# The second product of a fused attention and MoE kernel: from chunks of 512 tokens in one pass to chunks of 1024 tokens in two passes

## The chip, the cores and the metric

The kernel runs on one core of one Trainium2 chip. The metric is the time of one execution on the device in microseconds (us); the median of three runs before the change is 1302.53 us (1302.04 to 1304.47). Five engines work beside each other, each in its own program order: PE multiplies matrices into PSUM (eight banks of 128 x 512 fp32), VectorE (DVE), ScalarE (ACT) and GpSimd (POOL) work element by element, and SP issues the transfers between the chip's memory and SBUF.

## The reference

```python
def _moe_ref(x, w_in, w_out):                   # x: 4608 tokens x 512, from attention
    h = x @ w_in                                # 4608 x 2048
    sp = np.where(h > 20.0, h, np.log1p(np.exp(np.minimum(h, 20.0))))
    g = h * np.tanh(sp)                         # Mish
    return (g @ w_out).astype(np.float32)       # 4608 x 512
```

Ahead of it stands an attention over 8 batches, 8 heads and 576 positions that keeps only scores within tau of each row's maximum. All is fp32 at the door. The change touches only the last line, `g @ w_out`, and the preparation of `w_out`.

## The kernel before

**Three stages.** Attention and the first product (`x @ w_in`) run interleaved until 881 us or so; the last batch of the first product follows, beside the preparation of `w_out`; from 932 us on PE does the second product alone. The change concerns this last stage, and the preparation ahead of it.

**Number format.** An fp32 factor is held as two fp32r tiles, an upper part (a CAST on ACT) and the rest (a subtraction on DVE). A product is three matmuls: upper by upper, upper by rest, rest by upper. So `gh` and `gl` are the two parts of g, `w2h` and `w2l` of w_out, `sh` and `sl` of sums of w_out's blocks.

**The second product** (lines 966 to 1015) is a loop of `NG` = 72 steps n = (chunk c, j). Step j takes two blocks of 128 hidden features, j and j + 8. The output is made transposed: 512 output features by tokens. Chunk 0 (n < 8) is a plain product of 512 tokens: 24 matmuls of 512 moving columns a step, four banks. Each of the chunks 1 to 8 also has 512 tokens, as two halves of 256; with two halves of the features and two of the output this is a 2 x 2 by 2 x 2 block product, done in Winograd's way with seven products (`PRODUCTS`) in place of eight. Each product is 256 output features by 256 tokens: two groups of 128, three matmuls of 256 moving columns each, into one bank. So a step is 42 matmuls, and seven of the eight banks are in use. `leave` (line 935) takes each product out of its bank at j = 7, when its sum is complete, with running sums in SBUF tiles `c`, and writes four quarters of the output.

**What a step prepares for later steps**, ahead of its own matmuls in each engine's program order (lines 968 to 976):

- `combine(n + 3)`: ACT applies Mish to the loaded h in `z`; DVE makes two differences of 128 x 256 in one instruction, POOL two more of 128 x 256 after it.
- `split_z(n + 2)`: ACT casts seven blocks (128 x 1792) to `gh`, DVE subtracts to `gl`. Three pairs of tiles are used in turn, so this waits until PE has ended step n - 1.
- `load_z(n + 6)`: SP loads z, 2 transfers of 256 KB, into one of five buffers.

**The preparation of w_out**, for j = 0 to 7: `load_w` (two transfers), `convert`, `compose` (DVE and POOL join the two words of the 64 bit numbers), `upper_w` (one ACT cast of 128 x 1024), `lower_w` (one DVE subtraction of 128 x 1024), `sums_w` and `split_w`.

Instructions on PE, DVE, ACT and POOL stand in the order in which the code makes them (class `InOrder`); SP's order is set by the scheduler. Nearly all of them are recorded at line 77, so the profile's rows are told apart by tile names.

Of the kernel before, what the change touches and what calls it, by code (L numbers as in the profile page):

```python
# [62 lines left out]
def fv(ap):  # L63
    return ap.bitcast(F32)
# [78 lines left out]
def attention_moe(tc, q, k, v, tau, w_in, w_out, out):  # L143
# [3 lines left out]
    with ExitStack() as outer:  # L147
# [22 lines left out]
        def scratch(i, name):  # L170

            if i < 3:
                return homes["zp"].tile([P, 2048], F32, name=name, tag=f"b{(i + 1) % 3}")
            return homes["er"].tile([P, 2048], F32, name=name, tag=f"b{i}")

        def load_w(j):
            y = scratch(j % 3, "w").bitcast(U32)
            words[j] = y.rearrange("p (n t) -> p n t", t=2)
            for e in range(2):
                f = j + e * NJ  # L180
                nc.sync.dma_start(
                    words[j][:, e * DM:(e + 1) * DM],
                    w_out[f * P:(f + 1) * P].bitcast(U32).rearrange("p (n t) -> p n t", t=2),
                )

        def convert(j):
# [3 lines left out]

        def compose(j):
            top, low = words[j][:, :, 1], words.pop(j)[:, :, 0]
            wa[j] = [homes["wr"].tile([P, 4 * QT], F32R, name=f"w2h{j}")]
            a, b = (homes["wr"].tile([P, 4 * QT], U32, name=n, tag=f"{n}l{j}") for n in "as")
            whole[j] = fv(b)
            nc.vector.tensor_scalar(fv(b), fv(top), TOP_MAX, -TOP_MAX, ALU.min, ALU.max)
            nc.vector.tensor_scalar(a, b, 3, 0x7FFFFFF8, ALU.logical_shift_left, ALU.bitwise_and)
            nc.vector.scalar_tensor_tensor(b, b, 0x80000000, a, ALU.bitwise_and, ALU.bitwise_or)
            nc.gpsimd.tensor_tensor(b, b, low, ALU.add)

        def upper_w(j):
            nc.scalar.copy(wa[j][0], whole[j])

        def lower_w(j):
            wa[j].append(homes["wr"].tile([P, 4 * QT], F32R, name=f"w2l{j}", tag=f"al{j}"))
            nc.vector.tensor_tensor(wa[j][1], whole[j], fv(wa[j][0]), ALU.subtract)

        def sums_w(j):
            y = z[j]
            a11, a21, a12, a22 = (whole[j][:, i * QT:(i + 1) * QT] for i in range(4))  # L210
            nc.vector.tensor_tensor(y[:, 4], a21, a22, ALU.add)
            nc.vector.tensor_tensor(y[:, 6], a21, a11, ALU.subtract)
            nc.vector.tensor_tensor(y[:, 5], y[:, 4], a11, ALU.subtract)
            nc.vector.tensor_tensor(y[:, 7], a12, y[:, 5], ALU.subtract)

        def split_w(j):
# [5 lines left out]
            nc.scalar.copy(ws[j][0], y)  # L222
            nc.vector.tensor_tensor(ws[j][1], y, fv(ws[j][0]), ALU.subtract)

        def load_z(n):
            if n < NG:
                c, j = divmod(n, NJ)
                z[n] = scratch(CYCLE[n % 5], "z").rearrange("p (n t) -> p n t", t=QT)
                if c == 0:
                    for i in range(2):  # L230
                        nc.sync.dma_start(z[n][:, i:4:2], hd[i][:, j])
                else:
                    for at, i in ((0, 2 * c + 1), (2, 2 * c)):
                        nc.sync.dma_start(z[n][:, at:at + 2], hd[i][:, j])

        def combine(n):
            if n < NG:
                y = z[n]
                nc.scalar.activation(y[:, :4], y[:, :4], AF.Mish)
                if n >= NJ:  # L240
                    nc.vector.tensor_tensor(
                        y[:, 4:6], y[:, :1].to_broadcast([P, 2, QT]), y[:, 1:3], ALU.subtract
                    )
                    nc.gpsimd.tensor_tensor(y[:, 6], y[:, 1], y[:, 5], ALU.subtract)
                    nc.gpsimd.tensor_tensor(y[:, 7], y[:, 6], y[:, 3], ALU.subtract)

        def split_z(n):
            if n < NG:
                home = homes[("er", "wl", "wl")[n % 3]]
                gs[n] = [home.tile([P, 7, QT], F32R, name=f"g{m}", tag=f"g{m}{n % 3}") for m in "hl"]  # L250
                y = z[n][:, :4] if n < NJ else z.pop(n)[:, 1:]
                to = [x[:, :4] if n < NJ else x for x in gs[n]]
                nc.scalar.copy(to[0], y)
                nc.vector.tensor_tensor(to[1], y, fv(to[0]), ALU.subtract)

        nc = Engines(tc)
        with ExitStack() as first:
# [671 lines left out]
        def held():  # L929
            pair = hp.tile([P, 2, 2, QT], F32, name="c", tag="hst")  # L930
            return pair[:, 0], pair[:, 1]

        sums = {}

        def leave(k, c, o):

            def put(value, n, half):
                at = (2 * c + half) * QT
                nc.sync.dma_start(places[:, 2 * n:2 * n + 2, at:at + QT], value)

            def add(to, a, b, op=ALU.add):
                nc.vector.tensor_tensor(to, a, b, op)

            if k == 0:
                sums["c"], sums["u"] = held()
                nc.scalar.copy(sums["c"], o)
            elif k == 1:
                add(sums["u"], o, sums["c"])
            elif k == 2:
                sums["v"], sums["value"] = held()  # L950
                add(sums["v"], o, sums["u"])
            elif k == 3:
                add(sums["value"], o, sums["v"])
                put(sums["value"], 1, 1)
                add(sums["u"], o, sums["u"])
            elif k == 4:
                add(sums["u"], o, sums["u"])
                put(sums["u"], 0, 1)
            elif k == 5:
                add(sums["v"], sums["v"], o, ALU.subtract)  # L960
                put(sums["v"], 1, 0)
            else:
                add(sums["c"], o, sums["c"])
                put(sums["c"], 0, 0)

        for n in range(NG):
            c, j = divmod(n, NJ)
            combine(n + 3)
            for i in range(n + 1 + (n > 0), n + 3):
                split_z(i)  # L970
# [3 lines left out]
                split_w(i)  # L974
            for i in range(n + 5 + (n > 0), n + 7):
                load_z(i)
            if j == 0:
                banks = [bank("o") for _ in range(4 if c == 0 else len(PRODUCTS))]
            if c == 0:
                gh, gl = (x.rearrange("p n t -> p (n t)") for x in gs.pop(n))  # L980
                wh, wlo = wa[j]
                order = [(e, d) for e in range(2) for d in range(ND)]
                if j == NJ - 1:
                    order.sort(key=lambda at: at[1])
                for e, d in order:
                    cols = slice(2 * e * QT + d * P, 2 * e * QT + (d + 1) * P)
                    toks = slice(2 * e * QT, 2 * (e + 1) * QT)
                    for i, (x, y) in enumerate(((wh, gh), (wh, gl), (wlo, gh))):
                        nc.tensor.matmul(
                            banks[d], x[:, cols], y[:, toks],  # L990
                            start=j == e == i == 0, stop=j == NJ - 1 and e == 1 and i == 2,
                        )
                    if j == NJ - 1 and e == 1:
                        if d % 2 == 0:
                            pair = [x.rearrange("p n t -> p (n t)") for x in held()]
                        value = pair[d % 2]
                        if d % 2:
                            nc.vector.tensor_copy(value, banks[d])
                        else:
                            nc.scalar.copy(value, banks[d])  # L1000
                        nc.sync.dma_start(out[d * P:(d + 1) * P, :2 * QT], value)
                continue
            for k, (wi, gi) in enumerate(PRODUCTS):
                o = banks[k].rearrange("p (n t) -> p n t", t=QT)
                w, at = (wa[j], (0, 2, 3)[wi]) if wi < 3 else (ws[j], wi - 3)
                for b in range(2):
                    cols = slice(at * QT + b * P, at * QT + (b + 1) * P)
# [54 lines left out]
```

## Time and profile before

| what | value |
|---|---|
| the profiled execution, time | 1302.35 us |
| its span | 1300.6 us |
| granted TensorE clock | 1.00 |
| second product, first to last matmul | 931.97 to 1295.29 us |
| chunks 1 to 8 of it | from 978.27 us |
| DMA traffic over the span | 163 GB/s |

Of the 1.75 us between span and time the profile shows nothing. A row of the timeline gives start, duration, engine, line, operation, output <- inputs and form; idle time ahead of it and what ended that stand in brackets. A matmul's duration is the way of one through the array; they overlap, so that the distance of starts is the rate. A row of the windows gives for each engine the busy time and the number of instructions.

### The profile page before, as it was taken

How to read it: one execution, taken by the hardware profiler on the slowest of the kernel's cores; microseconds unless marked ns; L12 is line 12 of the kernel's file. 1: busy time of each engine (PE TensorE's matmuls, PEld its weight loads, DVE VectorE, ACT ScalarE, POOL GpSimd, SP SyncE). 2: the span in 40 equal slices, each digit the busy share in tenths (PEclk: the TensorE clock that was granted, in tenths of full speed). 3: DMA queues.
4: the chain of work that ended last, by engine and by line, in shares of the span. 5: the costliest groups of instructions: out<-in, count | busy, mean ns of one | idle time of the engine just before them, and what ended most of it. 6: DMA issues, size and time to landing. Idle time of an engine off the chain costs nothing.

```text
span 1300.6 us, 28613 instructions
## 1 busy us (share of the span) xinstructions
PE 1269.9 (98%) x9761; PEld 1137.0 (87%) x9761; DVE 991.5 (76%) x2590; ACT 842.4 (65%) x1620; POOL 776.2 (60%) x1071
## 2 busy tenths in 40 slices
PE   8789999999999999999999999999999999999998
PEld 6446998898888889889888888989889999999998
DVE  5888867777787888888888788859976676666664
ACT  5887877777866666676676666645755555655552
POOL 3778897787776786686677678624313433344331
PEclk9999999999999999999999999999999999999999
DMA  6444564777556566566655656547644444344440
GB/s 182 124 145 124 153 188 132 209 212 230 153 172 204 175 177 197 162 181 202 181 185 177 208 164 188 158 139 245 208 140 136 143 134 136 116 138 142 135 131 33
DMA packets 168802, 213.26 MB, mean 164 GB/s; under 512 B 27088, under 2 KB 140496, under 8 KB 163536
## 3 DMA queue, kind: packets, MB, share of 16 engines
q1 hardware_dynamic: 168656, 211.44, 53.4%
q8 instruction: 77, 1.26, 0.4%
q14 instruction: 69, 0.57, 0.1%
HBM read 151.62 MB, written 59.77 MB: 163 GB/s over the span
## 4 chain that ended last, share of the span: by engine, by line
PE 80%; DVE 8%; ACT 5%; issue 3%; POOL 2%; DMA 1%; DVEq 0%; POOLq 0%; ACTq 0%; SPq 0%
PE o L77 27%; PE h L77 22%; PE y L77 11%; PE s L77 10%; PE tp L77 8%; DVE st L77 3%; ACT e L77 2%; DVE p L77 1%; PE t L77 1%; DVE w2l L77 1%; DVE hst L77 1%; DVE s L77 1%; ACT dec L77 1%; ACT xh L77 0%; DVE a L77 0%
## 5 line engine op out<-in xcount | busy, mean ns | idle before, releaser
L77 DVE SCALAR_TENSOR_TENSOR p<-s,st,e 128x576 f32<-128x576 f32 x288 | 234.6, 815 | 103.5 <-ACT e L77 101.6
L77 POOL TENSOR_SCALAR p<-p,st 128x576 f32<-128x576 f32 x288 | 244.6, 849 | 98.0 <-DVE st L77 73.4
L77 POOL TENSOR_TENSOR z<-z 128x256 f32<-128x256 f32 x128 | 124.4, 976 | 223.0 <-DVE z L77 214.2
L77 ACT ACTIVATE e<-s,st 128x576 f32<-128x576 f32 x288 | 215.7, 749 | 55.4 <-DVE st L77 52.4
L77 PE MATMUL s<-k,q 128*128 128x288 f32 (+1 forms) x1280 | 228.7, 326 | 13.9 <-DVE p L77 13.6
L77 DVE TENSOR_REDUCE st<-s 128x1 f32<-128x576 f32 x288 | 217.1, 754 | 26.4 <-PE s L77 25.8
L77 DVE TENSOR_TENSOR gl<-z,gh 128x1792 fp32r<-128x1792 f32 (+1 forms) x72 | 141.6, 1968 | 108.2 <-ACT gh L77 108.2
L77 ACT CAST gh<-z 128x1792 fp32r<-128x1792 f32 (+1 forms) x72 | 116.5, 1620 | 149.9 <-issue 81.1
L77 PEld LDWEIGHTS s<-k,q 128*128 128x128 f32 (+1 forms) x1280 | 169.7, 188 | 45.4 <-DVE p L77 33.4
L77 PE MATMUL h<-xh,w1h 128*128 128x288 f32 x624 | 188.8, 302 | 0.0
L77 PE MATMUL h<-xl,w1h 128*128 128x288 f32 x624 | 184.2, 295 | 0.0
L77 PE MATMUL h<-xh,w1l 128*128 128x288 f32 x624 | 183.8, 295 | 0.0
L77 PE MATMUL tp<-ident,p 128*128 128x128 f32 x1152 | 175.2, 275 | 5.1 <-POOL p L77 3.6
L77 PE MATMUL h<-xh,wt 128*128 128x288 f32 x640 | 156.5, 305 | 3.4 <-ACT hst L77 3.4
L77 PEld LDWEIGHTS tp<-ident,p 128*128 128x128 f32 x1152 | 137.1, 140 | 24.5 <-issue 7.8
L77 PE MATMUL o<-gh,sl 128*128 128x256 f32 x512 | 144.5, 282 | 0.0
L77 PE MATMUL o<-gl,sh 128*128 128x256 f32 x512 | 143.8, 281 | 0.0
L77 PE MATMUL o<-gh,sh 128*128 128x256 f32 x512 | 143.5, 280 | 0.0
L77 PE MATMUL y<-hi,vf 128*64 128x320 f32 (+1 forms) x512 | 139.6, 413 | 0.0
L77 PE MATMUL y<-lo,vf 128*64 128x320 f32 (+1 forms) x512 | 139.6, 413 | 0.0
L77 ACT COPY hi<-tp 128x512 f32<-128x512 f32 (+1 forms) x160 | 87.2, 545 | 78.0 <-PE tp L77 76.3
L77 PE MATMUL o<-gl,w2h 128*128 128x256 f32 (+1 forms) x448 | 133.3, 298 | 1.3 <-DVE gl L77 1.3
(79 smaller groups left out, 3215.8 us busy)
## 6 DMA issues: line engine op xcount, KB each, us to landing
wt<-sw SPq DMA_DIRECT2D x40, 1024.0 KB, 5.9
z<-hd SPq DMA_DIRECT2D x144, 256.0 KB, 3.1
r<-q SPq DMA_DIRECT2D x108, 160.0 KB, 2.3
r<-k SPq DMA_DIRECT2D x108, 160.0 KB, 2.7
hd<-hst SPq DMA_DIRECT2D x60, 256.0 KB, 6.0
vf<-v SPq DMA_DIRECT2D x64, 160.0 KB, 3.5
out_t<-c SPq DMA_DIRECT2D x36, 256.0 KB, 2.4
dec<-w_in SPq DMA_DIRECT2D x16, 512.0 KB, 3.9
```

Source lines behind the costliest of these rows:

```text
L77: made = method(*args, **kwargs)
```

## The change

Chunks 1 to 4 of 1024 tokens take the place of chunks 1 to 8 of 512. Each token half now has 512 tokens, so a product is 256 output features by 512 tokens and needs two banks: 14 banks in all, of eight. The seven products are therefore done in two passes over the eight j, first four (`PASSES[0]`, the early pass), then three (`PASSES[1]`, the late pass). Products 5 and 6 of the late pass are added in PSUM onto what products 3 and 0 of the early pass left in theirs, so these four banks are kept; the other four are emptied between the passes. The number of steps stays 72: an early step has 24 matmuls of 512 columns, a late one 18.

An early step needs three of the four blocks of z (768 KB in four transfers) and four operands, a late one four blocks (1024 KB in four transfers) and three operands; Mish and the combination run for both passes. In an early combine DVE makes one difference of 128 x 512 and POOL two after it; in a late one POOL makes two and DVE a sum after them. The fourth operand's rest in an early step has a tile of its own, `ge`, and a DVE instruction of its own. `leave` now works on halves of a bank, 128 x 256, in SBUF tiles that held the upper parts of one quarter of w_out (`w2q`), which is not needed after step 7; product 6 is copied out by ACT into three `value` tiles. w_out is loaded in four transfers for each j, its upper part made by two ACT casts, its rest by DVE (768 columns) and POOL (256).

```diff
-PRODUCTS = ((0, 1), (4, 5), (5, 3), (3, 4), (6, 0), (2, 6), (1, 2))
+PASSES = (((0, 0, 2), (1, 4, 1), (2, 5, 0), (3, 3, 3)), ((4, 6, 0), (5, 2, 1), (6, 1, 2)))
...
         def upper_w(j):
-            nc.scalar.copy(wa[j][0], whole[j])
+            nc.scalar.copy(wa[j][0], whole[j][:, QT:])
+            nc.scalar.copy(wa[j][1], whole[j][:, :QT])
...
-            nc.vector.tensor_tensor(wa[j][1], whole[j], fv(wa[j][0]), ALU.subtract)
+            nc.vector.tensor_tensor(low[:, QT:], whole[j][:, QT:], fv(hi), ALU.subtract)
+            nc.gpsimd.tensor_tensor(low[:, :QT], whole[j][:, :QT], fv(quarter), ALU.subtract)
...
+        def place(n):
+            c, r = divmod(n - NJ, 2 * NJ)
+            return (c, *divmod(r, NJ))
...
+        def combine(n):
+            if NJ <= n < NG:
+                y = z[n]
+                if place(n)[1]:
+                    nc.scalar.activation(y, y, AF.Mish)
+                    nc.gpsimd.tensor_tensor(y[:, 0], y[:, 1], y[:, 0], ALU.subtract)
+                    nc.gpsimd.tensor_tensor(y[:, 2], y[:, 2], y[:, 3], ALU.subtract)
+                    nc.vector.tensor_tensor(y[:, 2], y[:, 2], y[:, 0], ALU.add)
                 else:
+                    nc.scalar.activation(y[:, :3], y[:, :3], AF.Mish)
+                    nc.vector.tensor_tensor(y[:, 3], y[:, 0], y[:, 2], ALU.subtract)
+                    nc.gpsimd.tensor_tensor(y[:, 0], y[:, 0], y[:, 1], ALU.subtract)
+                    nc.gpsimd.tensor_tensor(y[:, 1], y[:, 1], y[:, 3], ALU.subtract)
...
+            if place(n)[1]:
+                gs[n] = [[x[:, i] for i in range(3)] for x in (gh, gl)]
+                nc.scalar.copy(gh[:, :3], y[:, 1:])
+                nc.vector.tensor_tensor(gl, y[:, 1:], fv(gh[:, :3]), ALU.subtract)
+                return
...
+            nc.scalar.copy(gh, y)
+            nc.vector.tensor_tensor(gl, y[:, :3], fv(gh[:, :3]), ALU.subtract)
+            nc.vector.tensor_tensor(extra[n % 3], y[:, 3], fv(gh[:, 3]), ALU.subtract)
...
+        def leave(k, b, c, o):
+            for h in range(2):
+                x = o[:, h * QT:(h + 1) * QT]
+                us, vs = ("u", b, h), ("v", b, h)
...
+                if k == 0:
+                    kept[us] = spare(2 * b + h)
+                    nc.scalar.copy(kept[us], x)
+                elif k == 1:
+                    add(kept[us], x, kept[us])
+                elif k == 2:
+                    kept[vs] = spare(4 + 2 * b + h)
+                    add(kept[vs], x, kept[us])
+                elif k == 3:
+                    add(kept[vs], x, kept[vs])
+                    put(kept[vs], 1, 1)
+                    add(kept[us], x, kept[us])
+                elif k == 4:
+                    add(kept[us], x, kept[us])
+                    put(kept[us], 0, 1)
+                elif k == 5:
+                    add(kept[vs], kept[vs], x, ALU.subtract)
+                    put(kept[vs], 1, 0)
+                else:
+                    value = wl.tile([P, QT], F32, name="value", bufs=3)
+                    nc.scalar.copy(value, x)
+                    put(value, 0, 0)
...
+            if n == NJ:
+                eight = [[bank("o") for _ in range(2)] for _ in range(4)]
+                roles = [0, 1, 2, 3]
+            elif late == j == 0:
+                roles = [roles[i] for i in (2, 1, 3, 0)]
+            for k, wi, gi in PASSES[late]:
+                o = eight[roles[{4: 1, 5: 3, 6: 0}.get(k, k)]]
                 for b in range(2):
...
                     for i, (x, y) in enumerate(((0, 0), (0, 1), (1, 0))):
                         nc.tensor.matmul(
-                            o[:, b], w[x][:, cols], gs[n][y][:, gi],
-                            start=j == b == i == 0, stop=j == NJ - 1 and b == 1 and i == 2,
+                            o[b], weight(j, x, wi + 1, b * P) if wi < 3 else ws[j][x][:, cols], gs[n][y][gi],
+                            start=j == i == 0 and k < 5, stop=j == NJ - 1 and i == 2,
+                            skip_group_check=True,
                         )
-                if j == NJ - 1:
-                    leave(k, c, o)
+                    if j == NJ - 1:
+                        leave(k, b, c, o[b])
```

DVE at the end of a chunk, before the change: `z` are the differences of `combine`, `gl` the rests of `split_z`, `o` banks and `c` running sums.

```order
L77 TENSOR_TENSOR z_16899<-z_16899 128x512
L77 TENSOR_TENSOR gl_17055<-z_16846,gh_17054 128x1792
L77 TENSOR_TENSOR z_16952<-z_16952 128x512
L77 TENSOR_TENSOR gl_17108<-z_16899,gh_17107 128x1792
L77 TENSOR_TENSOR c_17120<-o_16737,c_17120 128x512
L77 TENSOR_TENSOR c_17135<-o_16738,c_17120 128x512
L77 TENSOR_TENSOR c_17135<-o_16739,c_17135 128x512
L77 TENSOR_TENSOR c_17120<-o_16739,c_17120 128x512
```

DVE at the end of an early pass, after the change: `o_145..` are banks, `o_154..` and `o_155..` the running sums in SBUF; the two banks of product 1 are 14586 and 14587, of product 2 14590 and 14591, of product 3 14584 and 14585.

```order
L77 TENSOR_TENSOR z_15313<-z_15313 128x512
L77 TENSOR_TENSOR gl_15423<-z_15275,gh_15422 128x1536
L77 TENSOR_TENSOR z_15351<-z_15351 128x512
L77 TENSOR_TENSOR gl_15460<-z_15313,gh_15459 128x1536
L77 TENSOR_TENSOR o_15471<-o_14586,o_15471 128x256
L77 TENSOR_TENSOR o_15473<-o_14586,o_15473 128x256
...
L77 TENSOR_TENSOR o_15495<-o_14590,o_15471 128x256
...
L77 TENSOR_TENSOR o_15495<-o_14584,o_15495 128x256
L77 TENSOR_TENSOR o_15471<-o_14584,o_15471 128x256
```

Seven additions of 128 x 512 once in 512 tokens have become 16 of 128 x 256 here and 8 more at the end of the late pass, once in 1024 tokens; as before they stand behind the combination for step n + 3 and the rest for step n + 2.

PE across the first seam between an early and a late pass, after the change, with the engine whose semaphore a matmul waits for: the last rows of step 15 (product 3), then products 4 and 5 of step 16.

```order
L77 MATMUL o_14591<-gh_14772,sh7_14475 128x512
L77 MATMUL o_14591<-ge_14470,sh7_14475 128x512
L77 MATMUL o_14591<-gh_14772,sl7_14476 128x512
L77 MATMUL o_14586<-gh_14810,sh0_14211 128x512 [waits DVE_49]
L77 MATMUL o_14586<-gl_14811,sh0_14211 128x512
...
L77 MATMUL o_14587<-gh_14810,sh0_14211 128x512 [waits DVE_49]
...
L77 MATMUL o_14590<-gh_14810,w2h0_13544 128x512 [waits DVE_49]
```

In this first chunk product 1 was in 14586 and 14587, product 3 in 14590 and 14591: product 4 starts anew in the banks of product 1 and waits for their additions, product 5 goes on in those of product 3 and waits for theirs. Before the change a chunk's first product found a free bank, the eighth, and no two products shared one.

ACT at the very end, after the change, where `value` are the three tiles of product 6.

```order
L77 CAST gh_16866<-z_16756 128x1536
L77 CAST gh_16888<-z_16787 128x1536
L77 COPY value_16959<-o_14584 128x256
L77 COPY value_16962<-o_14584 128x256
L77 COPY value_16968<-o_14585 128x256
L77 COPY value_16971<-o_14585 128x256
```

The last of the four copies takes the tile of the first again; before, the last work ahead of the final transfer was one DVE addition of 128 x 512.

More of the change, by code (lines that the diff above doesn't have):

```diff
@@ L178, in load_w @@
             words[j] = y.rearrange("p (n t) -> p n t", t=2)
-            for e in range(2):
-                f = j + e * NJ
+            for to, e, h in ((0, 0, 1), (1, 0, 0), (2, 1, 0), (3, 1, 1)):
+                rows, cols = slice((j + e * NJ) * P, (j + e * NJ + 1) * P), slice(h * QT, (h + 1) * QT)
                 nc.sync.dma_start(
-                    words[j][:, e * DM:(e + 1) * DM],
-                    w_out[f * P:(f + 1) * P].bitcast(U32).rearrange("p (n t) -> p n t", t=2),
+                    words[j][:, to * QT:(to + 1) * QT],
+                    w_out[rows, cols].bitcast(U32).rearrange("p (n t) -> p n t", t=2),
                 )
@@ L236, in combine @@
[L236 to L245, printed above, removed]
@@ L247, in split_z @@
-        def split_z(n):
[L248 to L254, printed above, removed]
+            if NJ <= n < NG:
+                c, late, j = place(n)
+                z[n] = scratch(CYCLE[n % 5], "z").rearrange("p (n t) -> p n t", t=2 * QT)
+                for q in range(2):
+                    cols = slice(q * QT, (q + 1) * QT)
+                    nc.sync.dma_start(z[n][:, :2, cols], hd[4 * c + 4 + q][:, j])
+                for q in range(2):
+                    cols = slice(q * QT, (q + 1) * QT)
+                    if late:
+                        nc.sync.dma_start(z[n][:, 2:, cols], hd[4 * c + 2 + q][:, j])
+                    else:
+                        nc.sync.dma_start(z[n][:, 2, cols], hd[4 * c + 2 + q][:, j, 0])
+            elif n < NJ:
+                z[n] = scratch(CYCLE[n % 5], "z").rearrange("p (n t) -> p n t", t=QT)
+                for i in range(2):
+                    nc.sync.dma_start(z[n][:, i:4:2], hd[i][:, n])
@@ new lines, in attention_moe @@
+        extra = []
+        def split_z(n):
+            if n >= NG:
+                return
+            home = homes[("er", "wl", "wl")[n % 3]]
+            gh = home.tile([P, 4, 2 * QT], F32R, name="gh", tag=f"gh{n % 3}")
+            gl = home.tile([P, 3, 2 * QT], F32R, name="gl", tag=f"gl{n % 3}")
+            if n < NJ:
+                y = z[n][:, :4].rearrange("p n t -> p (n t)")
+                gs[n] = [x.rearrange("p n t -> p (n t)")[:, :4 * QT] for x in (gh, gl)]
+                nc.scalar.copy(gs[n][0], y)
+                nc.vector.tensor_tensor(gs[n][1], y, fv(gs[n][0]), ALU.subtract)
+                return
+            y = z.pop(n)
+            if place(n)[1]:
+                gs[n] = [[x[:, i] for i in range(3)] for x in (gh, gl)]
+                nc.scalar.copy(gh[:, :3], y[:, 1:])
+                nc.vector.tensor_tensor(gl, y[:, 1:], fv(gh[:, :3]), ALU.subtract)
+                return
+            if not extra:
+                for _ in range(2):
+                    made = hp.tile([P, 2, 2 * QT], F32R, name="ge", tag="hst")
+                    extra.extend(made[:, i] for i in range(2))
+            gs[n] = [[gh[:, i] for i in range(4)], [gl[:, i] for i in range(3)] + [extra[n % 3]]]
+            nc.scalar.copy(gh, y)
+            nc.vector.tensor_tensor(gl, y[:, :3], fv(gh[:, :3]), ALU.subtract)
+            nc.vector.tensor_tensor(extra[n % 3], y[:, 3], fv(gh[:, 3]), ALU.subtract)
@@ L927, in attention_moe @@
         places = out.rearrange("(n p) t -> p n t", p=P)
[L929 to L964, printed above, removed]
@@ L966, in attention_moe @@
         for n in range(NG):
-            c, j = divmod(n, NJ)
             combine(n + 3)
@@ L976, in attention_moe @@
                 load_z(i)
[L977 to L981, printed above, removed]
+            if n < NJ:
+                j = n
+                if j == 0:
+                    banks = [bank("o") for _ in range(4)]
+                gh, gl = gs.pop(n)
                 order = [(e, d) for e in range(2) for d in range(ND)]
```

57 lines of the change are left out of this document (33 added, 24 removed).

## The prediction

> **What bounds the kernel now.** I read the page first, then the chain of work that ended last, then the busy time in stretches of the second product, then single rows.
>
> ```profile
> PE 1269.9 (98%) x9761; PEld 1137.0 (87%) x9761; DVE 991.5 (76%) x2590; ACT 842.4 (65%) x1620; POOL 776.2 (60%) x1071
> 939.48 352.56 PE o L77 x2825
> 1057.00:1096.50 39.50, 39.50 (x337) 39.50 (x337) 26.45 (x24) 21.58 (x17) 15.83 (x16) 1.00 0.43 134
> ```
>
> PE is busy for 98% of the span, and the chain's longest piece is 352.56 us of the second product without a break. In the stretch (one old chunk; the pairs are busy time and count of PE, PEld, DVE, ACT, POOL) PE is busy throughout, DVE for 67%, ACT 55%, POOL 40%, at full clock. So only two things can change the time here: what a matmul costs, and a new wait of PE.
>
> **Change, term 1: the rate of the matmuls.** The distance of starts is read from PE's timeline: a stretch of chunk 0 with 512 columns, then chunks 1 to 8 with 256.
>
> ```profile
> 939.82 0.39 PE L77 MATMUL o<-gh,w2l 128*128 128x512 f32 x1
> 940.05 0.39 PE L77 MATMUL o<-gh,w2h 128*128 128x512 f32 x1
> ...
> 948.22 0.39 PE L77 MATMUL o<-gh,w2l 128*128 128x512 f32 x1
> ...
> 970.18 0.39 PE L77 MATMUL o<-gl,w2h 128*128 128x512 f32 x1
> ...
> 972.90 0.39 PE L77 MATMUL o<-gl,w2h 128*128 128x512 f32 x1
> ...
> 978.27 0.28 PE L77 MATMUL o<-gh,w2h 128*128 128x256 f32 x1
> ...
> 1295.29 0.28 PE L77 MATMUL o<-gh,w2l 128*128 128x256 f32 x1
> ```
>
> Of chunk 0's 192 matmuls 166 start from 939.82 up to the first of 256 columns: 38.45 us, 231.6 ns each. The fastest stretch, 12 matmuls from 970.18 to 972.90, has 226.7; the common distance elsewhere is 233.3 (8.17 us for the 35 from 940.05 to 948.22). The 2688 of 256 columns have 2687 distances in 317.02 us: 118.0 ns. The change makes 1344 of 512 columns out of them (32 pairs of an early and a late step, 24 + 18 matmuls): 1344 x 231.6 = 311.3 against 2688 x 118.0 = 317.2 us, **a gain of 5.9 us**; from 3.6 (at 233.3) to 12.5 (at 226.7).
> Beside it a rule: the Trainium skill, page "TensorE: Matmul & The Clock Gate", section "Wait — 56ns, not 53.3ns?", gives N / 2.4 GHz plus about 2.5 ns for the distance of warm matmuls. Here both lengths are slower than that, so the trace disagrees with it; by it the gain would be an estimated 3.4 us, and the total below 2.5 us higher.
>
> **Term 2: DVE and POOL on each other's time.** These rows show what an instruction with two SBUF inputs does while the other engine has one.
>
> ```profile
> 895.94 1.22 DVE L77 TENSOR_TENSOR w2l<-s,w2h 128x1024 fp32r<-128x1024 f32 x1
> 896.15 3.30 POOL L77 TENSOR_TENSOR s<-s,w 128x1024 uint32<-128x1024 uint32 x1 [4.54 <-DVE s L77]
> 902.13 2.46 POOL L77 TENSOR_TENSOR s<-s,w 128x1024 uint32<-128x1024 uint32 x1 [2.68 <-DVE s L77]
> 902.28 3.39 DVE L77 TENSOR_TENSOR w2l<-s,w2h 128x1024 fp32r<-128x1024 f32 x1
> 1109.61 2.02 DVE L77 TENSOR_TENSOR gl<-z,gh 128x1792 fp32r<-128x1792 f32 x1
> 1111.54 1.22 DVE L77 TENSOR_TENSOR z<-z 128x512 f32<-128x512 f32 x1
> 1117.06 0.68 DVE L77 TENSOR_TENSOR z<-z 128x512 f32<-128x512 f32 x1
> 1117.82 1.56 POOL L77 TENSOR_TENSOR z<-z 128x256 f32<-128x256 f32 x2 [2.94 <-DVE z L77]
> 32.78 1.27 POOL L77 TENSOR_TENSOR w1l<-dec,w1h 128x512 fp32r<-128x512 f32 x1 [0.24 <-ACT w1h L77]
> L77 DVE TENSOR_TENSOR hst<-h,hst x200: 436/458/460, 354.8 to 881.3; 128x288 f32<-128x288 f32 x100
> ```
>
> The same DVE subtraction takes 1.22 us at 895.94 and 3.39 at 902.28, where POOL began 0.15 us earlier: it ends at 905.67, 1.08 us after POOL's end at 904.59. POOL at 896.15 in its turn ends 2.29 us after DVE's end. So such instructions do not run side by side; the later one waits whole, and about 0.14 us of it is hidden in the hand-over (1.22 - 1.08). An addition with a PSUM input is not drawn in: the 200 of the last row never take more than 0.46 us, in stretches in which POOL works much.
>
> Durations for the change: DVE 128 x 512 0.68 us (row of 1117.06), 0.60 from start to start; 128 x 1792 1.93 from start to start (1109.61 to 1111.54); so 1.04 ns an element, and 128 x 1536 1.66 (alone 1.76). POOL 128 x 512: 1.27. A pair of steps has three of the first, two of the second and four of POOL's:
> - nothing hidden: 3 x 0.60 + 2 x 1.66 + 4 x 1.27 = 10.2 us;
> - every hand-over hidden: 3 x 0.54 + 2 x 1.62 + 4 x 1.13 = 9.4 us.
>
> PE needs 42 x 0.2316 = 9.73 us for a pair. Before, two steps took 2 x (0.60 + 1.93 + 1.56) = 8.2 of 9.9 us. Late steps alone: 4.4 to 4.8 us against PE's 18 x 0.2316 = 4.17; early ones 5.0 to 5.4 against 5.56. So **late passes fall behind by 0.2 to 0.6 us a step**, 2 to 5 us a pass, and early ones win back about as much. The operands' lead is two steps at most, since `split_z(n + 2)` waits for step n - 1; that bears the loss inside a pass. I take no wait of PE inside passes (price 0; with nothing hidden 32 x (10.2 - 9.7) = 15 us more), but a lead that is one split shorter at the seams.
>
> **Term 3: the seams.** There DVE has its additions behind that queue. The length of 128 x 256 instructions, the additions of an old chunk, and the load of an old step are in these rows:
>
> ```profile
> 953.03 0.75 DVE L77 TENSOR_TENSOR z<-s 128x256 f32<-128x256 f32 x2
> 953.70 0.42 DVE L77 TENSOR_TENSOR z<-z,s 128x256 f32<-128x256 f32 x1
> 1135.78 3.67 DVE L77 TENSOR_TENSOR c<-o,c 128x512 f32<-128x512 f32 x5
> L77 DVE TENSOR_TENSOR gl<-z,gh 128x1792 fp32r<-128x1792 f32 x54 | 111.0, 2056 | 84.8 <-ACT gh L77 84.8
> L77 ACT CAST gh<-z 128x1792 fp32r<-128x1792 f32 x54 | 91.3, 1691 | 122.8 <-issue 62.8 <-POOL z L77 56.7 <-PE o L77 3.3
> L77 ACT ACTIVATE z<-z 128x1024 f32<-128x1024 f32 x52 | 54.9, 1055 | 0.0
> ```
>
> Two of 128 x 256 lie between 953.03 and 953.70, 0.335 us from start to start; I take it for an addition with a bank, too.
>
> - *Early to late, four times.* From the start of the last early step, one split late: DVE does `gl` of n + 1 (1.62), waits for a POOL instruction (1.13), combines n + 3 (0.54), does `gl` of n + 2 (1.62): 4.9 us. Then 12 additions (products 1, 2 and half of 3) before product 5 may enter product 3's bank: 4.0, so 8.9. PE wants that bank after 24 + 6 matmuls, at 6.95: **2.0 us of waiting**. On time (the first `gl` done before) the additions follow the matmuls closely and nothing is waited for; with one more POOL instruction between it is 3.1.
> - *Late to early, three times.* DVE has `gl` and `ge` of n + 1 (1.62 + 0.54), the combination (0.54), `gl` and `ge` of n + 2 (2.16), two POOL instructions between (2.26): 7.1; two additions (0.67) free the first bank of product 4, which product 1 needs at 4.17 + 1.39 = 5.56. **2.2 us**; 0 if on time, 3.4 with one POOL instruction more.
>
> Sum 4 x 2.0 + 3 x 2.2 = 14.6 us; ends 0 and 23. I take the middle values because the shared time is 97% to 105% of PE's, and before, at 83%, DVE idled only 1.6 us a step ahead of `gl` (84.8 us in the 54 of the row).
>
> **Term 4: the tail.**
>
> ```profile
> 1296.30 0.68 DVE L77 TENSOR_TENSOR c<-o,c 128x512 f32<-128x512 f32 x1
> out_t<-c SPq DMA_DIRECT2D x36, 256.0 KB, 2.4
> L77 ACT COPY x<-y 128x256 f32<-128x256 f32 x32 | 11.9, 372 | 6.4 <-PE y L77 6.3
> ```
>
> The last matmul starts at 1295.29 and ends 0.28 later; the final addition ends at 1296.98, 1.4 us behind it, and the final transfer follows. Now ACT's fourth copy needs the first copy's tile, whose transfer (2.4 us by the row, half as large here) starts about when PE ends; then 0.37 for the copy: 2.8 us. **1.4 us more**; 0 if the smaller transfer takes 1 us, 3 if SP's queue of twelve issues holds the last ones.
>
> **At nothing:**
>
> ```profile
> z<-hd SPq DMA_DIRECT2D x144, 256.0 KB, 3.1
> 939.48 0.50 PE L77 MATMUL o<-gl,w2h 128*128 128x512 f32 x1 [1.30 <-DVE gl L77]
> ```
>
> ACT: from 1.055 for Mish and 1.69 for a cast of 1792 (0.83 ns an element more or less) a pair has Mish 1.48 + 1.91, casts 1.90 + 1.48, and copies 0.37: 7.1 of 9.73 us; uncovered it would cost only where it delays the seams. Transfers: 1792 KB of z a pair in place of 1024, so about 217 in place of 134 GB/s and 70% in place of 43% of the transfer engines; z is issued some two steps ahead of its use and lands in 3.1 us, so 5 us would be hidden too. Preparation of w_out: DVE saves 0.27 us a j, POOL adds 0.78, beside PE's first product; PE's one longer wait for it is the 1.30 us of the row, so -1.3 to about +1.5 us; I take 0.
>
> **Sum**, against the profiled execution's 1302.35 us (0.2 under the median of the runs): -5.9 + 14.6 + 1.4 = +10.1, so **1312.5 us**.
>
> **Rivals.**
> - *The seams hold* (faster): DVE reaches its additions on time, as it did before. For it: before, five additions in a row left PE without a wait. Against it: the shared time, 83% then, about 100% now. Time: 1302.35 - 5.9 + 1.4 = 1297.9, and 1291 at 226.7 ns. It decides whether the first addition starts before about 2.9 us after the start of the last early step (6.95 less 4.0).
> - *They hold in part*: about half of 14.6, at the better rates: 1302 to 1305, no difference that a measurement tells (0.2%, 2.6 us).
> - *DVE and POOL are the bound throughout*: 15 us inside the passes, and half of the seams on top: 1302.35 - 5.9 + 15 + 7.3 + 1.4 = 1320; about 1326 with all of them.
> - *The change does not do what it says*: 512 columns cost twice 256 in the new order, at 236 ns; then term 1 is 0 and the time 1318.4.
>
> **How the numbers follow.** My forecast, waits at the seams, 0.43; bound throughout 0.20; no gain in the rate 0.05; in part 0.14; seams hold 0.18. So faster 0.18, same 0.14, slower 0.68. The range leaves out the better half of the first rival and the upper half of the third: 1297.5 to 1323.
>
> **What would show it.** PE's distances of 227 to 233 ns inside a pass; breaks of about 2 us ahead of product 5 in each first late step and ahead of product 1 in each first early step, ended by DVE's additions; almost no idle time of DVE in late passes, and POOL rows of 2 us and more. I am wrong if PE has no breaks at the seams, if it waits for `gl` inside passes, or if breaks end by a transfer.

## The result, and the profile after

The changed kernel takes 1322.25 us (median of four runs, 1321.43 to 1322.87), the kernel before 1302.28 on the same chip: a ratio of 1.0149, 95% interval 1.0132 to 1.0167, so slower by 20 us, 1.5%. The time lies inside the range, at its upper edge. The profiled execution took 1322.24 us, with a span of 1320.5 (before 1302.35 and 1300.6).

The page of the changed kernel, busy time first, then the chain that ended last and its costliest group:

```profile
PE 1273.8 (96%) x8417; PEld 1076.3 (82%) x8417; DVE 1035.1 (78%) x2664; ACT 890.0 (67%) x1654; POOL 891.4 (68%) x1079
...
PE 71%; DVE 9%; ACT 6%; issue 6%; DMA 4%; POOL 3%; SPq 1%; DVEq 0%; POOLq 0%; ACTq 0%
...
L77 POOL TENSOR_TENSOR z<-z 128x512 f32<-128x512 f32 x128 | 231.4, 1821 | 137.0 <-DVE z L77 80.5
```

PE has 1344 instructions fewer but is busy 4 us longer, and POOL's 128 x 512 takes 1821 ns on average, where 1.27 us was its time alone. Where PE stops is seen in its timeline at the first early to late seam. The late pass begins at 1022.43, and product 5 needs product 3's two banks:

```profile
1022.43 0.39 PE L77 MATMUL o<-gh,sh 128*128 128x512 f32 x1
...
1023.58 0.40 PE L77 MATMUL o<-gh,sl 128*128 128x512 f32 x1
1025.43 0.50 PE L77 MATMUL o<-gh,w2h 128*128 128x512 f32 x1 [1.45 <-DVE o L77]
...
1026.75 0.50 PE L77 MATMUL o<-gh,w2h 128*128 128x512 f32 x1 [0.37 <-DVE o L77]
```

DVE and POOL at the same place, from their timelines:

```profile
1014.39 0.69 DVE L77 TENSOR_TENSOR z<-z 128x512 f32<-128x512 f32 x1 [1.19 <-POOL z L77]
1015.00 2.85 DVE L77 TENSOR_TENSOR gl<-z,gh 128x1536 fp32r<-128x1536 f32 x1
1019.04 0.69 DVE L77 TENSOR_TENSOR z<-z 128x512 f32<-128x512 f32 x1 [1.20 <-POOL z L77]
1019.64 1.75 DVE L77 TENSOR_TENSOR gl<-z,gh 128x1536 fp32r<-128x1536 f32 x1
1021.31 5.38 DVE L77 TENSOR_TENSOR o<-o 128x256 f32<-128x256 f32 x16
...
1014.93 4.08 POOL L77 TENSOR_TENSOR z<-z 128x512 f32<-128x512 f32 x2 [0.57 <-ACT z L77]
```

POOL has its two subtractions from 1014.93 to 1019.01. In that time `gl` takes 2.85 us in place of 1.75, and the late combination waits for POOL until 1019.04. So the 16 additions begin at 1021.31. Twelve of them (0.336 us each) must end before product 5 enters product 3's first bank, 1.39 us after the pass's start: PE waits unless they begin 2.64 us ahead of it (12 x 0.336 - 1.39). They begin 1.12 ahead, which gives a wait of 1.5; the row has 1.45.

The first late to early seam, PE's rows and one of DVE:

```profile
1058.10 0.40 PE L77 MATMUL o<-gh,w2h 128*128 128x512 f32 x1
...
1059.26 0.39 PE L77 MATMUL o<-gh,w2l 128*128 128x512 f32 x1
1061.96 0.50 PE L77 MATMUL o<-gh,sh 128*128 128x512 f32 x1 [2.31 <-DVE o L77]
...
1062.91 0.63 PE L77 MATMUL o<-gh,sh 128*128 128x512 f32 x1
1063.34 0.63 PE L77 MATMUL o<-gl,sh 128*128 128x512 f32 x1
...
1065.90 0.44 PE L77 MATMUL o<-gl,sh 128*128 128x512 f32 x1
1066.17 0.39 PE L77 MATMUL o<-gh,sl 128*128 128x512 f32 x1
...
1061.16 2.72 DVE L77 TENSOR_TENSOR o<-o 128x256 f32<-128x256 f32 x8
```

Product 1 waits 2.31 us for two additions into which DVE comes at 1061.16, 3.06 us after the pass's start where 0.72 would have done (1.39 less two of 0.336). And a second thing stands there: from 1062.91 the matmuls are 0.43 us apart. The windows show why (columns: busy time and count of PE, PEld, DVE, ACT, POOL, then the granted clock, the share of the transfer engines and GB/s):

```profile
1058.00:1060.00 2.00, 1.64 (x8) 1.00 (x6) 2.00 (x2) 0.62 (x2) 2.00 (x1) 1.00 0.71 206
1060.00:1062.00 2.00, 0.04 (x1) 0.04 (x1) 2.00 (x4) 0.00 (x0) 1.92 (x2) 1.00 0.90 275
1062.00:1064.00 2.00, 2.00 (x6) 1.62 (x7) 1.89 (x6) 0.74 (x2) 0.37 (x1) 0.64 0.77 255
1064.00:1066.00 2.00, 2.00 (x6) 1.52 (x6) 0.69 (x1) 2.00 (x2) 0.09 (x1) 0.51 0.79 258
1066.00:1068.00 2.00, 2.00 (x10) 1.63 (x9) 1.06 (x1) 2.00 (x2) 1.92 (x2) 1.00 0.69 218
```

Once PE had stood for 2.3 us, the clock fell to half for some 3.3 us. PE counts as busy in this time, which is why its busy time grew. Five of the seven seams show it.

All of the difference, from PE's starts in the two kernels (chunks from 978.27 to 1295.29 before, from 978.08 to 1313.68 after). A wait here is the distance of two starts less 0.233 us, some 0.16 longer than the idle time in brackets. A seam's waits are added up (1.62 and 0.53 at the first), at most seams with the 0.1 us by which the second start behind a break is late, too:

| part | us |
|---|---|
| rate of the 512-column matmuls (231.6 ns between starts less than 0.34 us apart) | -6.0 |
| four early to late waits: 2.15, 2.79, 2.28, 2.14 | +9.4 |
| three late to early waits: 2.58, 2.42, 2.39 | +7.3 |
| matmuls at half clock behind five of these | +7.9 |
| tail from the last matmul's start to the end, 5.3 before, 6.8 after | +1.5 |
| chunks begin earlier | -0.2 |
| sum (spans: 1320.5 - 1300.6) | +19.9 |

The 231.6 ns still hold a few starts that are late behind a break. The 1278 distances without any delay have 231.2 ns, which is -6.5; the waits and the half clock are then 0.5 more.

### The profile page after: what moved, and what is told of

It reads as the page before. It is cut to its first block, busy times and chain, and to the rows that moved or that the text cites. A ratio compares the mean times of both kernels' runs of the same rounds, so it can differ in the third digit from the quotient of the medians.

```text
span 1320.5 us, 26462 instructions
## 1 busy us (share of the span) xinstructions
PE 1273.8 (96%) x8417; PEld 1076.3 (82%) x8417; DVE 1035.1 (78%) x2664; ACT 890.0 (67%) x1654; POOL 891.4 (68%) x1079
## 4 chain that ended last, share of the span: by engine, by line
PE 71%; DVE 9%; ACT 6%; issue 6%; DMA 4%; POOL 3%; SPq 1%; DVEq 0%; POOLq 0%; ACTq 0%
PE h L77 22%; PE o L77 18%; PE y L77 11%; PE s L77 10%; PE tp L77 8%; DMA z<-hd 3%; DVE st L77 2%; ACT e L77 2%; DVE gl L77 2%; PE t L77 1%; DVE p L77 1%; DMA w<-w_out 1%; POOL z L77 1%; DVE ge L77 1%; DVE o L77 1%
## 5 line engine op out<-in xcount | busy, mean ns | idle before, releaser
L77 POOL TENSOR_TENSOR z<-z 128x512 f32<-128x512 f32 x128 | 231.4, 1821 | 137.0 <-DVE z L77 80.5
L77 ACT CAST gh<-z 128x2048 fp32r<-128x2048 f32 (+2 forms) x72 | 116.6, 1621 | 111.0 <-PE o L77 58.1
L77 DVE TENSOR_TENSOR gl<-z,gh 128x1536 fp32r<-128x1536 f32 (+1 forms) x72 | 137.5, 1911 | 34.2 <-ACT gh L77 34.2
L77 DVE TENSOR_TENSOR hst<-h,hst 128x288 f32<-128x288 f32 x200 | 89.6, 453 | 43.9 <-PE h L77 39.2
L77 POOL TENSOR_TENSOR k<-r,k 128x320 fp32r<-128x320 f32 x108 | 94.4, 874 | 41.3 <-ACT k L77 40.6
L77 POOL TENSOR_TENSOR q<-r,q 64x320 fp32r<-64x320 f32 x108 | 95.6, 885 | 37.8 <-ACT q L77 14.1
L77 ACT ACTIVATE z<-z 128x1536 f32<-128x1536 f32 (+2 forms) x72 | 117.2, 1628 | 5.1 <-DMA z<-hd 5.0
```

The source lines that it names most:

```text
L77: made = method(*args, **kwargs)
```

## The experiments

Theory: the sharing between DVE and POOL holds DVE up ahead of the seams, PE waits for its additions there, and the clock falls behind the breaks. Rivals: DVE's additions themselves are too many, the transfers of z are late, or the order of the products alone is at fault. "Stage" is the time from the first chunk's first matmul to the last matmul's start, from PE's timeline of the profiled run. A ratio is to the kernel before on the same chip; order_465, one_pool, dve_465 and before_dve ran on another chip, where the kernel before takes 1301.85 us.

| kernel | median us | ratio to before (95%) | stage us |
|---|---|---|---|
| before | 1302.28 | | 317.0 |
| changed | 1322.25 | 1.0149 (1.0132 to 1.0167) | 335.6 |
| all_dve | 1302.76 | 1.0001 (0.9992 to 1.0010) | 315.9 |
| idle_pool | 1356.68 | 1.0413 (1.0396 to 1.0431) | 370.2 |
| keep_busy | 1319.29 | 1.0123 (1.0108 to 1.0138) | 331.9 |
| order_645 | 1318.25 | 1.0112 (1.0097 to 1.0128) | 332.8 |
| order_465 | 1316.44 | 1.0111 (1.0095 to 1.0126) | 330.4 |
| one_pool | 1309.42 | 1.0055 (1.0041 to 1.0069) | 321.7 |
| dve_465 | 1297.09 | 0.9965 (0.9953 to 0.9978) | 310.5 |
| before_dve | 1301.91 | 1.0001 (0.9992 to 1.0010) | 317.0 |

### all_dve: POOL's four subtractions go to DVE

```diff
-                    nc.gpsimd.tensor_tensor(y[:, 0], y[:, 1], y[:, 0], ALU.subtract)
-                    nc.gpsimd.tensor_tensor(y[:, 2], y[:, 2], y[:, 3], ALU.subtract)
+                    nc.vector.tensor_tensor(y[:, 0], y[:, 1], y[:, 0], ALU.subtract)
+                    nc.vector.tensor_tensor(y[:, 2], y[:, 2], y[:, 3], ALU.subtract)
...
```

> POOL's two subtractions of each combination are done by DVE. Theory (DVE and POOL exclude each other, so the additions at the seams come late): the exclusive time of a pair falls from 9.4 to 10.2 us to 7 x 0.60 + 2 x 1.66 = 7.5 of PE's 9.73; the waits ahead of product 1 (7.3 us in all) vanish, those ahead of product 5 (9.4 us) shrink by a third or more, and the half clock behind them mostly goes: 1301 to 1308 us. Rival (the additions are simply too many for DVE): DVE has 2.7 us more to do a pair, the waits grow: 1324 to 1332. Rival (the transfers of z are late): no change, 1321 to 1323.

1302.76 us, 19.5 less than the changed kernel. The profiled execution took 1306.23 us; what it is longer by lies ahead of the chunks, which begin at 982.22 in place of 978.08. DVE's rows at the first seam, PE's next to them, and DVE's at the second:

```profile
1022.81 1.76 DVE L77 TENSOR_TENSOR gl<-z,gh 128x1536 fp32r<-128x1536 f32 x1 [1.73 <-ACT gh L77]
1024.48 5.39 DVE L77 TENSOR_TENSOR o<-o 128x256 f32<-128x256 f32 x16
...
1026.57 0.39 PE L77 MATMUL o<-gh,sh 128*128 128x512 f32 x1
...
1028.60 0.50 PE L77 MATMUL o<-gh,w2h 128*128 128x512 f32 x1 [0.48 <-DVE o L77]
...
1061.69 2.73 DVE L77 TENSOR_TENSOR o<-o 128x256 f32<-128x256 f32 x8
```

The additions now begin 2.09 us ahead of the late pass, 0.97 earlier than with POOL, and PE's wait is 0.97 shorter (1.45 to 0.48). The next early pass starts at 1061.27, the additions 0.42 after it, inside the 0.72: no wait. The clock stays at 1.00. Three groups of DVE, in the changed kernel and then in all_dve, show where the time came from:

```profile
L77 DVE TENSOR_TENSOR gl<-z,gh 128x1536 fp32r<-128x1536 f32 x62 | 123.9, 1998 | 29.1 <-ACT gh L77 29.1
L77 DVE TENSOR_TENSOR z<-z 128x512 f32<-128x512 f32 x61 | 48.0, 787 | 53.1 <-POOL z L77 48.1 <-DMA z<-hd 2.7 <-ACT z L77 2.4
L77 DVE TENSOR_TENSOR ge<-z,gh 128x512 fp32r<-128x512 f32 x31 | 51.8, 1671 | 0.0
...
L77 DVE TENSOR_TENSOR gl<-z,gh 128x1536 fp32r<-128x1536 f32 x62 | 108.8, 1755 | 28.1 <-ACT gh L77 28.0
L77 DVE TENSOR_TENSOR z<-z 128x512 f32<-128x512 f32 x183 | 123.3, 688 | 5.5 <-ACT z L77 2.1
L77 DVE TENSOR_TENSOR ge<-z,gh 128x512 fp32r<-128x512 f32 x30 | 20.5, 684 | 0.0
```

DVE does three times as many combinations in 75 us more, and gets 48 us of waiting for POOL, 31 us of longer `ge` and 15 us of longer `gl` back. The additions and the transfers are the same as in the changed kernel, and some 20 us of PE's waits and half clock (335.6 to 315.9) are gone all the same, so these two rivals fall.

### idle_pool: as all_dve, with work on POOL that nobody needs

```diff
+                    for _ in range(2 if extra else 0):
+                        nc.gpsimd.tensor_tensor(extra[3], y[:, 1], y[:, 1], ALU.subtract)
...
+                    for _ in range(2 if extra else 0):
+                        nc.gpsimd.tensor_tensor(extra[3], y[:, 2], y[:, 2], ALU.subtract)
```

> As all_dve, but POOL still does two subtractions of 128 x 512 a step, of a block of z by itself into a tile that nobody reads, so nobody waits for their result; only the memory ports are used as before. Theory (exclusion): most of what all_dve gained is lost again, 1314 to 1325. Rival (it was POOL's latency as a link in the chain from z to the operands, not the exclusion): as all_dve, within 1.5 us of it.

1356.68 us, more than expected. No engine waits for these results, yet DVE's instructions become longer, and PE stops for 5 us at the seams. DVE's groups, then POOL's (its `ge` is the tile that nobody reads), then PE's row at the first late to early seam:

```profile
L77 DVE TENSOR_TENSOR z<-z 128x512 f32<-128x512 f32 x183 | 175.2, 971 | 3.7 <-ACT z L77 0.4
L77 DVE TENSOR_TENSOR gl<-z,gh 128x1536 fp32r<-128x1536 f32 x62 | 135.4, 2185 | 0.0
...
L77 POOL TENSOR_TENSOR ge<-z 128x512 fp32r<-128x512 f32 x122 | 188.5, 1545 | 170.3 <-ACT z L77 164.2 <-POOL ge L77 0.8
...
1072.73 0.79 PE L77 MATMUL o<-gh,sh 128*128 128x512 f32 x1 [5.01 <-DVE o L77]
```

So the time in turn is enough to make the waits, without any wait for POOL's result. What that wait adds in the changed kernel (48.1 us of DVE's idle time in the group above) this run does not tell apart. The prediction's own durations give the size only with every hand-over hidden: DVE here has all seven operations of 128 x 512 in a pair of steps, and POOL four more, 7 x 0.54 + 2 x 1.62 + 4 x 1.13 = 11.5 us where PE needs 9.73, or 58 us in 32 pairs; the stage grew by 54.3 over all_dve. With nothing hidden it is 12.6 us and 92 us. That is the case in which the sharing binds throughout: DVE never waits ahead of `gl` (0.0), but PE waits for `gl` inside late passes.

### one_pool: only the later subtraction of each step goes to DVE

```diff
-                    nc.gpsimd.tensor_tensor(y[:, 2], y[:, 2], y[:, 3], ALU.subtract)
+                    nc.vector.tensor_tensor(y[:, 2], y[:, 2], y[:, 3], ALU.subtract)
...
-                    nc.gpsimd.tensor_tensor(y[:, 1], y[:, 1], y[:, 3], ALU.subtract)
+                    nc.vector.tensor_tensor(y[:, 1], y[:, 1], y[:, 3], ALU.subtract)
```

> One of POOL's two subtractions of each step (the later one) goes to DVE, the other stays on POOL. Theory (the waits grow with the time that DVE and POOL have in turn): POOL holds DVE up half as long, the early to late waits fall to about 1.2 us as in all_dve, and late to early ones to between nothing and 1.2 us, below what halves the clock: 1303 to 1309. Rival (any work of POOL beside DVE holds up the last copies, since it is one wait for POOL that counts, not the sum): 1316 to 1322.

1309.42 us, 0.4 above the expected range. Early to late waits are as in all_dve (0.48 and 0.36), but the three late to early ones stay at 1.6 to 1.7, more than expected:

```profile
1061.05 0.50 PE L77 MATMUL o<-gh,sh 128*128 128x512 f32 x1 [1.63 <-DVE o L77]
...
1062.00:1066.00 4.00, 4.00 (x19) 3.23 (x18) 2.54 (x6) 3.81 (x4) 1.30 (x1) 1.00 0.74 243
```

The clock stays at 1.00 behind this break. Two, one and no operations on POOL give 1322, 1309 and 1303 us: the loss follows the amount, though 7.9 us of the first step down is the half clock.

### keep_busy: PE repeats a matmul at the seams in place of standing

The first matmul into product 4's first bank in a late pass, and into product 0's in an early one from the second chunk on, is done eleven times in place of once.

```diff
-                    for i, (x, y) in enumerate(((0, 0), (0, 1), (1, 0))):
+                    seam = j == b == 0 and n > NJ and k == (4 if late else 0)
+                    for i, (x, y) in enumerate(((0, 0),) * (10 if seam else 0) + ((0, 0), (0, 1), (1, 0))):
+                        i = i - 10 if seam else i
...
-                            start=j == i == 0 and k < 5, stop=j == NJ - 1 and i == 2,
+                            start=j == 0 and i <= 0 and k < 5, stop=j == NJ - 1 and i == 2,
```

Each repeat starts the bank's sum anew, so the result stays the same.

> The first matmul into product 4's first bank (first late step) and into product 0's first bank (first early step of chunks 2 to 4) is done eleven times in place of once, so that PE works where it waited; 70 matmuls or 16.2 us of added work. Theory (the half clock follows the break in PE's work): the waits of 16.7 us take up the repeats, and the 7.9 us of half clock go: 1313 to 1317, granted clock 1.00 throughout. Rival (the half clock comes with the seam for another reason): 1321 to 1324 with the slow matmuls still there. If the waits did not take the repeats up: 1338.

1319.29 us, higher than expected. The same stretch as above, with repeats:

```profile
1058.00:1060.00 2.00, 2.00 (x10) 1.61 (x9) 2.00 (x2) 1.27 (x4) 1.33 (x1) 1.00 0.30 96
1060.00:1062.00 2.00, 2.00 (x10) 1.68 (x9) 2.00 (x3) 0.00 (x0) 1.92 (x2) 1.00 0.96 308
1062.00:1064.00 2.00, 1.99 (x9) 1.21 (x9) 2.00 (x7) 0.24 (x1) 1.10 (x1) 1.00 0.73 246
```

No half clock is left at any seam: with PE kept busy it does not fall. The gain is small because the repeats take 70 x 0.2316 = 16.2 us and some waits stay beside them (1.59, 0.80 and 0.71 us at three seams), together 4 us more than the 16.7 that PE stood before; 7.9 less 4 is what the stage shows (335.6 to 331.9).

### order_645: the late pass in another order

```diff
-PASSES = (((0, 0, 2), (1, 4, 1), (2, 5, 0), (3, 3, 3)), ((4, 6, 0), (5, 2, 1), (6, 1, 2)))
+PASSES = (((0, 0, 2), (1, 4, 1), (2, 5, 0), (3, 3, 3)), ((6, 1, 2), (4, 6, 0), (5, 2, 1)))
-                roles = [roles[i] for i in (2, 1, 3, 0)]
+                roles = [roles[i] for i in (2, 0, 1, 3)]
```

> In the late pass product 6 goes first (its bank waits only for ACT's copies), then 4, then 5; in the next chunk product 1 takes product 6's banks, 2 those of 4, 3 those of 5. Nothing is done less, but the additions have 1.39 us more before product 5 and 1.39 more before a bank of product 4 is wanted. Theory: the waits fall by up to 1.39 us at each of 7 seams, so by 5 to 10 us, and part of the half clock goes with them: 1309 to 1316. Rival (PE waits at the seams for operands, not for banks): no change, 1320 to 1324.

1318.25 us, above the expected 1309 to 1316. Product 5 is third now, and the late passes fall to some 34.3 us. But a new wait comes in: the next product 1 takes product 6's banks, and ACT's fourth copy waits until the first `value` tile is written out. ACT's rows and PE's:

```profile
1057.65 0.91 ACT L77 COPY value<-o 128x256 f32<-128x256 f32 x3
1063.25 0.37 ACT L77 COPY value<-o 128x256 f32<-128x256 f32 x1 [4.69 <-DMA out_t<-value]
...
1063.67 0.50 PE L77 MATMUL o<-gh,sh 128*128 128x512 f32 x1 [4.24 <-ACT value L77]
```

### order_465 and dve_465: the order that frees the banks in the order of need

```diff
-PASSES = (((0, 0, 2), (1, 4, 1), (2, 5, 0), (3, 3, 3)), ((4, 6, 0), (5, 2, 1), (6, 1, 2)))
+PASSES = (((0, 0, 2), (1, 4, 1), (2, 5, 0), (3, 3, 3)), ((4, 6, 0), (6, 1, 2), (5, 2, 1)))
...
-                roles = [roles[i] for i in (2, 1, 3, 0)]
+                roles = [roles[i] for i in (2, 1, 0, 3)]
```

Order alone:

> The order 4, 6, 5 of dve_465 with POOL's subtractions left on POOL, so that order and engine are told apart. Theory (two separate causes: DVE's backlog from sharing with POOL holds the banks, and product 5 comes too soon): the wait ahead of product 5 goes (the second passes fall from 35.7 to 37.3 us to some 33.5, 12 us together with the half clock in them), while product 1 of the next chunk still waits some 2.4 us for DVE's backlog and runs at half clock behind it: 1322 - 12 = 1310, range 1306 to 1314. Rival (the whole loss is the shared time of DVE and POOL, and PE waits for it wherever the products stand): 1319 to 1323.

Order and all_dve together:

> As all_dve (all four subtractions on DVE), and the second pass takes its products in the order 4, 6, 5, so that product 5, whose bank DVE empties last, comes a product later, and the next chunk's products 1, 2, 3 take the banks of 4, 6, 5 in that order. Theory (what all_dve has left at the seams is the bank wait ahead of product 5, 0.65 + 0.52 us at each of four seams, 4.7 us): these go and nothing takes their place, 1302.8 - 4.7 = 1298.1, range 1296.5 to 1300; no matmul in the chunks waits over 0.3 us. Rival one: product 6's four ACT copies now fall in the middle of the last step, the fourth waits for the first value tile's transfer, and the next chunk's product 2 waits for it as product 1 did in order_645 (3.3 to 4.4 us with half clock behind it): 1306 to 1312. Rival two: DVE's copies, not the order, set the waits, and they only move to the next pass: 1302 to 1304.

Alone it gives 1316.44 us, a miss by 2 us. Late passes fall to 34.2 to 34.6 us as meant, but product 1 now waits 2.92, 2.17 and 3.38 us where the changed kernel had 2.31, 2.15 and 2.10, and product 4 once 1.66: part of what PE no longer waits for at one seam it waits for at the next, since DVE's backlog is still there. With POOL off the combination, dve_465 has no wait in any chunk and takes **1297.09 us**, faster than both kernels, though only by 0.4% against the kernel before. Its additions begin as late as in all_dve, 2.09 us ahead of the first late pass (1021.17 against 1023.26), so that it is the order that takes these last waits away. Its first chunk of 1024 tokens, pass by pass:

```profile
978.90:1023.20 44.30, 44.30 (x193) 36.04 (x192) 35.66 (x46) 29.95 (x22) 0.00 (x0) 1.00 0.68 210
1023.20:1056.60 33.40, 33.40 (x145) 27.03 (x145) 32.88 (x45) 25.15 (x18) 0.00 (x0) 1.00 0.68 213
```

PE is busy throughout while DVE has work for 98% of a late pass. The wait for a `value` tile is there, too, but hidden:

```profile
1058.38 0.37 ACT L77 COPY value<-o 128x256 f32<-128x256 f32 x1 [2.57 <-DMA out_t<-value]
```

It ends at 1058.75. Product 2, which needs that bank, is due 2.78 us after the pass's start at 1056.64, at 1059.42: a margin of 0.7 us.

### before_dve: the kernel before without POOL's subtractions, the control

```diff
-                    nc.gpsimd.tensor_tensor(y[:, 6], y[:, 1], y[:, 5], ALU.subtract)
-                    nc.gpsimd.tensor_tensor(y[:, 7], y[:, 6], y[:, 3], ALU.subtract)
+                    nc.vector.tensor_tensor(y[:, 6], y[:, 1], y[:, 5], ALU.subtract)
+                    nc.vector.tensor_tensor(y[:, 7], y[:, 6], y[:, 3], ALU.subtract)
```

> The kernel before with its two subtractions per step on DVE and none on POOL: the control. Theory (before, PE never waits for these operations, so it is the two-pass order with kept banks that turned the sharing of DVE and POOL into time): no change, 1301.5 to 1303.5. Rival (taking POOL off is worth time in any form of this stage, so that all_dve owes its gain to that and not to the seams): 1285 to 1298. Third way (DVE has no room for two more operations in a step of the kernel before): over 1306.

1301.91 us, no change. In the kernel before, POOL's work cost PE nothing; it is the changed kernel, with its seams, that made a cost of it.

## Why the prediction was right in direction, and where its size was off

The forecast was 1312.5 us, ten too low; the seams as the cause, and the direction, held.

- **Term 1, the rate: right.** -5.9 was forecast, -6.0 measured, or -6.5 without the small delays behind breaks. dve_465, which has no waits, shows it by itself: the stage takes 310.5 us in place of 317.0, -6.5. No rate rival is left, and in dve_465 the gain also reaches the time.
- **Term 2, the shared time: right.** Instructions of DVE and POOL take turns (`gl` 2.85 us beside POOL, 1.75 without), and PE does not wait for operands inside passes. The Trainium skill states it as a rule, page "SBUF — State Buffer", section "SBUF: two separate sides": an exclusive lock, held for a whole instruction, and not a shared bandwidth. The traces agree, idle_pool with 2185 ns for a `gl` of 1755 most plainly. The rival with DVE and POOL as the bound throughout came close in time (1320) for another reason: no pass of the changed kernel waits for operands, as idle_pool's do. (Its sum with all of the seams is 1327.5, not about 1326.)
- **One sign did not come.** "Almost no idle time of DVE in late passes" was forecast; over the first late pass DVE has work for 25.54 of 36 us:

```profile
1022.00:1058.00 36.00, 34.18 (x147) 27.19 (x146) 25.54 (x32) 24.40 (x17) 22.37 (x15) 1.00 0.60 189
```

  In the second late pass it stands three times until POOL's subtractions are done (2.70, 2.45 and 2.45 us) and once for ACT's cast (3.12). The additions still come about when forecast (at the first seam of each kind 4.4 us after the last early step's start, forecast 4.9, and 7.2 after the last late step's, forecast 7.1), but not because DVE's time was full.
- **Term 3, the seams: the mechanism right, the size 2 us low.** Both places, the engine and the instruction were as forecast: 4 x 2.0 + 3 x 2.2 = 14.6 us forecast, 9.4 + 7.3 = 16.7 measured. Ahead of product 5's first bank, the only one in the sum, it was 1.5 to 1.8 and not 2.0. Its second bank, which the sum left out, has a wait of its own of 0.5 at each early to late seam: four additions (1.34 us) stand between the two banks where PE has three matmuls (0.7). The step "on time (the first `gl` done before) ... nothing is waited for" was wrong: in all_dve the first `gl` is done before, and 1.2 us of waiting a seam stay: about 0.65 at the first bank, because the second `gl`, which stands ahead of the additions, waits 1.73 us for ACT's cast, and the 0.5 at the second. The price of one late split was therefore about 1.2 us on top of a wait that this order has without POOL's work, too.
- **What the sum lacked: 7.9 us.** It took PE's rate behind a break for that ahead of it. The clock halves behind five of seven breaks, and this is the largest part of the miss. keep_busy shows that it follows from PE's standing.
- **Term 4, the tail: the number right, in part by luck**, +1.4 forecast, +1.5 measured. The fourth copy waits for a transfer, as was said:

```profile
1315.19 2.89 SPq L990 DMA_DIRECT2D out_t<-value  x4
1317.35 0.37 ACT L77 COPY value<-o 128x256 f32<-128x256 f32 x1 [2.86 <-DMA out_t<-value]
```

  But SP issues the first of these transfers only at 1315.19, 1.5 us after the last matmul's start at 1313.68, and the copy ends at 1317.72, 4.0 us after it. Before, the final addition ended 1.7 us after the last matmul's start; so this part costs 2.3 and not 1.4. From there to the end it is 2.7 us in place of 3.6, which the sum did not have.
- **Terms at nothing.** What was priced at nothing (ACT, transfers, w_out) cost nothing that the traces show: no break of the chunks ends by a transfer, and they begin 0.2 us earlier.
- **The rival "the seams hold", 1297.9 us,** is about what the change is worth once its cause is removed: dve_465 has 1297.09.

## What to carry to other kernels

Work given to POOL is not free for DVE when both read two SBUF operands: add both engines' time against PE's, and if the sum is near it, try the work on DVE alone. At a seam between passes, count what stands in the emptying engine's queue ahead of the bank that is needed first, and let the next pass take banks in the order in which they come free. Price a break of about 2 us on PE higher than its length: here the half clock behind it cost half as much again.

## What the runs showed of the hardware that was not expected

The clock does not follow the length of a break alone. In the changed kernel a break of 1.66 us with one of 0.36 behind it (1110.27, 1111.59) left it at full speed, 1.34 with 0.36 (1279.73, 1281.06) did not. Of two rows of order_465 with the clock in the windows behind them, the longer break left it at full speed:

```profile
1061.90 0.50 PE L77 MATMUL o<-gh,sh 128*128 128x512 f32 x1 [2.92 <-DVE o L77]
...
1062.00:1066.00 4.00, 4.00 (x18) 3.24 (x19) 2.52 (x7) 2.88 (x3) 0.53 (x2) 1.00 0.94 296
...
1145.07 0.51 PE L77 MATMUL o<-gh,sh 128*128 128x512 f32 x1 [2.17 <-DVE o L77]
...
1146.00:1150.00 4.00, 4.00 (x13) 3.09 (x12) 2.51 (x6) 4.00 (x3) 1.76 (x2) 0.57 0.91 302
```

In the changed kernel one stretch of half clock lasts from about 1062.8 to 1066.1, some 3.3 us. The Trainium skill, page "TensorE: Matmul & The Clock Gate", gives a free-running window of 3413 ns (section "What's actually happening"), about this length, and in the section "HAM oscillation — how this bites in real kernels" the rule that gaps over some 3.4 us are to be avoided. By that rule none of these breaks would have cost any clock; the traces disagree, with falls behind breaks of 2.1 to 2.3 us, and behind two of about 1.4 with a second of 0.4 close to it. With the free-running window they agree. Worked out from the starts (the last, partly slow distance shared out between 0.427 and 0.231 us), the five stretches of the changed kernel end at 1065.99, 1151.33, 1199.12, 1236.67 and 1284.44: 85.34, 133.13, 170.68 and 218.45 us after the first, which is 25, 39, 50 and 64 times 3.413 within 0.03. So they lie on one grid, which does not begin with a break. On this grid each stretch follows an interval in which PE stood for 1.68 to 2.31 us in all; the two seams without one have at most 1.66 in an interval. The two stretches of order_465 end at 1149.55 and 1234.88, 25 times 3.413 apart; there the break of 2.92 us is cut by the grid into 1.82 and 1.10, and that of 2.17 lies in one interval. So the place of a break counts beside its length. A sharp limit does not come out, since 1.82 left the clock alone there and 1.68 did not here, and no run moved a break for this purpose.

An instruction moved from POOL to DVE also became shorter in itself: 128 x 512 takes POOL 1.27 us alone and DVE 0.69.
